# Wave 1 of an attention and MLP kernel: its casts, loads, weight sums and half products in another order

## The chip, the cores and the metric

One NeuronCore of a Trainium2 chip runs the kernel. Its engines work through instruction queues of their own, each in program order: TensorE (PE, matmuls), VectorE (DVE), ScalarE (ACT), GpSimd (POOL) and SyncE (SP, which here only issues DMAs). The metric is device time in microseconds of one execution. Before the change three runs took 203.18, 204.46 and 204.54 us; the median is 204.46.

## What is computed

Attention with a decay over 4 batches, 8 heads, 768 positions and 64 dimensions a head, then an MLP with a sigmoid GELU over the 3072 tokens:

```python
for b in range(nb):                                  # blocks of 64 positions
    intra = (q_b @ k_b^T * Dmask) @ v_b              # Dmask = lam ** (i - j), lower triangle
    inter = (q_b * lam_pow) @ kv_state
    out[:, :, block b] = intra + inter
    kv_state = lam_block * kv_state + (k_b * rev_pow)^T @ v_b
x = out as 3072 tokens x 512
h = x @ w_in                                         # 512 x 2048
g = h * sigmoid(1.702 * h)
out = g @ w_out                                      # 2048 x 512
```

## The kernel before

The sequence is cut into six waves of 128 positions (times 4 batches: 512 tokens a wave). For each wave the kernel loads k, q and v in two chunks c = 0, 1, scales and casts k and q to bf16 (`do_cast`), turns them (`turn_pe` through TensorE, `turn_dma` through SP's DMA transpose), computes scores, masks, outputs and state, and has the wave's attention output in `xT`. The first product of the MLP gives `h`, GELU gives `g_sb`, the second product (`product`, line 459) gives the output.

Both products of the later waves use a scheme with seven half products in place of eight (a Strassen-Winograd form). It needs sums and differences of halves of the inputs:

- `weight_sums(j)` (lines 421 to 426), for each of the four w_out chunks j: four VectorE instructions of 128x512 bf16. The first (t1) and the third (in place in w_out) read w_out alone, the second (t2) needs t1, the fourth (t4) needs t2.
- `g_sums` (line 439): s1 to s4 of `g_sb`, in a lower half (l) and an upper half (h), 128x1024 bf16 each.
- `in_sums` and `x_sums` (lines 518, 527) for the first product; "third" is an in-place one.

The second product's seven half products have numbers: 1 (raw inputs), 2, 3, 4 (t4), 5 (s1, t1), 6 (s2, t2), 7 (s3 and the in-place sum). Products 1, 6, 5, 3 add up in one PSUM bank, X; 2 goes to Q; 7 and 4 to V. Between 1, 6 and 5 the bank is copied to SBUF on ScalarE (`part`, line 472), so 6 and 5 may write X only when the copy before them is done; 4 waits likewise for the copy of 7; 3 waits until VectorE has read X after 5 (line 483).

The order of all work is written out by hand (`tc.manual_schedule`). Each engine runs its instructions in the order in which the program issues them. Wave 0 runs plain matmuls (fc 4 to fc 15 are `mlp1` calls, entries 3 to 14 of the list `main`), then half blocks of wave 1 (entries 15 to 22), then the steps of `STEPS[1]`. The list `side` says ahead of which entry of `main` the pieces of wave 1's attention and the sums are issued. In `STEPS`, `a1 a7 ...` and `b1 ...` are half products of the first product, `A2` and so on their GELUs, `P10` is product 1, half 0 (eight matmuls), `K0 tk0` the cast of k chunk 0 on GpSimd and its DMA transpose, `W2` the weight sums of chunk 2, `gl1` s1's lower half, `S0 M0 m1` scores and masks, `Lw` and `Lk` loads, `T1` a third `in_sums`. A minus sign means the wave before (in `STEPS[1]`: wave 0), a plus sign the wave after.

Three gates order DMAs. `gate_sync` issues a tiny DMA on SP that reads a weight chunk: it waits until the chunk has landed, and the loads behind it on SP wait with it. Wave 1's loads stand behind w_in chunk 2 (line 687), wave 2's k and q behind w_out chunk 2 (`next_loads`). `gate_pool` does the same on GpSimd: the w_out DMAs stand behind wave 1's q of chunk 1 (`weights_out`). In GpSimd's queue they also stand behind the cast of k of chunk 1, given to GpSimd in `side` at 12.

Of the kernel before, what the change touches and what calls it, by code (L numbers as in the profile page):

```python
# [25 lines left out]
def kernel(  # L26
# [13 lines left out]
    nc = tc.nc  # L40
# [379 lines left out]

    def weight_sums(j):
        b = w_out_sb[j].rearrange("p (m two) (c d) -> p two c m d", two=2, c=2)
        t1, t2, t4 = (t[:, j * CW // 2 : (j + 1) * CW // 2] for t in TS)
        for o, x, y in ((t1, b[:, 0, 1], b[:, 0, 0]), (t2, b[:, 1, 1], t1),
                        (b[:, 0, 1], b[:, 1, 1], b[:, 0, 1]), (t4, b[:, 1, 0], t2)):
            nc.vector.tensor_tensor(o, x, y, op=SUB)  # L426
# [136 lines left out]
    def one_step(w, s):  # L563
# [33 lines left out]
        elif s[0] == "X":  # L597
            x_sums(x)
        elif s[0] == "G":
            gate_pool(x_sum[w][3][0:1, 0, 0:1])  # L600
        elif s[0] == "g":
            m0, m1 = {"l": (0, 4), "h": (4, 8)}[s[1]]
            g_sums(w, m0, m1, tuple(int(c) - 1 for c in s[2:]))
        elif s[0] == "W":
            weight_sums(int(a))
        elif s[0] == "T":
            in_sums(int(a), True)
        elif s[0] == "L":
# [31 lines left out]
    with tc.manual_schedule():  # L640
# [42 lines left out]
        for j in range(3, len(IN_CH)):  # L683
            load_w_in(j)
        nc.gpsimd.affine_select(mask, mask, pattern=[[0, 1], [1, P]], channel_multiplier=-1, base=0,
                                compare_op=mybir.AluOpType.is_ge, fill=0.0)
        gate_sync(w_in_sb[2][0:1, 0, 0:2])
        load(1)
# [37 lines left out]
        def next_loads():  # L726
# [7 lines left out]
        side = [  # L734
            (0, end, 0, 1), (5, in_sums, 1), (6, in_sums, 2), (6.5, do_cast, 1, 0, "k", nc.vector), (7.5, in_sums, 3),
            (8.5, do_cast, 1, 0, "q", nc.vector), (9.5, turn_pe, 1, 0, "k"), (10.5, in_sums, 0),
            (11.5, turn_pe, 1, 0, "q"), (11.6, cast_v, 1, 0, (pool_copy, act_copy)),
            (12, do_cast, 1, 1, "k", nc.gpsimd), (12.6, scores, 0), (13, weights_out,), (13.1, next_loads,),
            (13.5, do_cast, 1, 1, "q", nc.vector), (13.6, one, 0), (14, turn_pe, 1, 1, "k"), (14.6, even, 0),
            (15, turn_pe, 1, 1, "q"), (15, end, 1, 0), (15, scores, 1), (16, cast_v, 1, 1, (act_copy, act_copy)),  # L740
            (16.5, one, 1), (17.5, even, 1), (17.6, g_sums, 0, 0, 4, (2,)), (17.7, g_sums, 0, 4, 8, (2,)),
            (18, end, 1, 1), (18.5, x_sums, 1), (18.6, in_sums, 3, True), (18.7, in_sums, 0, True),
            (19.5, weight_sums, 0), (20.5, weight_sums, 1),
        ]
# [38 lines left out]
```

## Time and profile before

The profiled execution took 202.9 us; its span from the first to the last instruction is 201.2 us.

| what | when or how long (us) |
|---|---|
| fc 4 starts, fc 15 ends | 20.64, 35.90 |
| wave 1's half blocks start, wave 1's first product starts | 39.99, 50.18 |
| wave 0's second product starts, its product 3 starts | 57.82, 72.04 |
| w_in chunks 1, 2, 3, 4 land | 17.82, 20.36, 22.86, 24.80 |
| wave 1's loads are issued; k, q, v of chunk 0 and k of chunk 1 land | 21.27; 26.34, 27.84, 29.34, 30.86 |
| w_out DMAs are issued; land | 33.53; 39.07, 42.15, 45.47, 48.01 |
| wave 2's loads are issued; GpSimd's casts of them | 46.19; 50.35 to 52.59 and 54.63 to 61.07 |
| wave 1's scores 0 (line 335) | 75.62 |

How to read the lines below. A timeline line gives the start, how long the group lasted, the engine, the line of the kernel, the operation, out<-in with the tiles' names, the shapes, and how many instructions of the kind followed each other; in brackets, how long the engine had been idle and who released it. The end of a matmul is modelled, so a wait reckoned from start to start is some 0.16 us longer than the bracket. Line 2 of the page is the busy share in 40 slices of about 5 us, in tenths, 9 for 90% or more.

### The profile page before, as it was taken

The numbers are of one execution on the slowest core, as the hardware profiler recorded it, in microseconds if no ns is written. First come the engines' busy times: TensorE is split into PE (matmuls) and PEld (weight loads), VectorE is DVE, ScalarE is ACT, GpSimd is POOL, SyncE is SP. The second block draws the span as 40 slices with busy tenths as digits, with TensorE's granted clock in tenths as the row PEclk, the third lists the DMA queues.
The fourth block names the chain that finished last, engine by engine and source line by source line (L and its number), as shares of the span: only waits on it lengthen the run. The fifth ranks groups of instructions, "written<-read, shape, count | busy, mean of one in ns | idle before, by whom it ended". The sixth has DMA issues, their size and how long they took to land.

```text
span 201.2 us, 5580 instructions
## 1 busy us (share of the span) xinstructions
PE 187.3 (93%) x2297; PEld 152.6 (76%) x2297; DVE 156.6 (78%) x293; ACT 130.8 (65%) x245; POOL 50.6 (25%) x73
## 2 busy tenths in 40 slices
PE   7999987779897889999999999999999999999993
PEld 2567534468775768888888888888988888888882
DVE  1797279767999784887979978979988799689860
ACT  4857667666791116647989548887559796487721
POOL 4564018200591000009600049200087000000000
PEclk9999999999999999999999999999999999999999
DMA  4999996999970798986799775699745831210013
GB/s 143 331 246 202 249 307 203 174 190 196 262 126 8 176 261 185 231 202 145 119 207 242 176 221 142 146 255 239 201 151 113 198 67 54 106 52 3 26 54 131
DMA packets 89603, 33.91 MB, mean 169 GB/s; under 512 B 67434, under 2 KB 89450, under 8 KB 89578
## 3 DMA queue, kind: packets, MB, share of 16 engines
q1 hardware_dynamic: 84680, 28.84, 57.7%
q0 software_dynamic: 4896, 4.72, 14.2%
q8 instruction: 18, 0.29, 0.6%
q14 instruction: 7, 0.06, 0.1%
q10 hardware_dynamic: 2, 0.00, 0.0%
HBM read 27.26 MB, written 6.29 MB: 167 GB/s over the span
## 4 chain that ended last, share of the span: by engine, by line
PE 70%; DVE 15%; DMA 6%; ACT 4%; POOL 2%; issue 1%; ACTq 0%; DVEq 0%
PE ps_X L459 20%; PE ps_hX L542 15%; PE ps_V L459 11%; PE ps_hV L542 7%; PE ps_Q L459 4%; DMA w_in<-in_moe_w_in_dram 4%; PE ps_hQ L542 4%; DVE w_out_t L426 4%; DMA kf<-in_k_dram 3%; DVE w_in_t L518 3%; PE ps_o L390 2%; PE ps_s L335 2%; PE ps_fill L147 2%; DVE qs L202 2%; DVE sm L267 1%; POOL ks L202 1%
## 5 line engine op out<-in xcount | busy, mean ns | idle before, releaser
L459 PEld LDWEIGHTS <-g_s 128*128 128x128 bf16 x384 | 37.1, 98 | 7.8 <-issue 2.9
L561 ACT ACTIVATE g_sb<-h_sb 128x512 bf16<-128x512 f32 x54 | 32.7, 633 | 1.4 <-DVE h_sb L550 1.4
L542 PEld LDWEIGHTS <-w_in 128*128 128x128 bf16 x288 | 28.2, 98 | 4.8 <-issue 1.5
L459 PEld LDWEIGHTS <-g_sb 128*128 128x128 bf16 x288 | 27.5, 98 | 5.0 <-issue 1.0
L221 ACT COPY part<-ps_hX 128x512 f32<-128x512 f32 x32 | 18.3, 588 | 10.3 <-PE ps_hX L542 10.3
L459 PE MATMUL ps_X<-w_out_t,g_s 128*128 128x256 bf16 x192 | 23.0, 273 | 0.7 <-ACT part L472 0.7
L542 PEld LDWEIGHTS <-w_in_t 128*128 128x128 bf16 x216 | 21.1, 98 | 2.5
L542 PE MATMUL ps_hX<-x_s,w_in_t 128*128 128x256 bf16 x144 | 21.6, 272 | 0.0
L439 DVE TENSOR_TENSOR g_s<-g_sb 128x1024 bf16<-128x1024 bf16 x24 | 16.2, 685 | 4.9 <-ACT g_sb L561 4.9
L209 POOL TENSOR_TENSOR ks<-kf,k_pow 128x512 bf16<-128x512 f32 x16 | 16.5, 1052 | 13.8 <-PE ps_h L414 13.8
L635 POOL CAST behind_q<-x_s 1x1 f32<-1x1 bf16 x3 | 0.5, 173 | 69.2 <-DVE x_s L527 69.2
L209 POOL TENSOR_TENSOR qs<-qf,q_pow 128x512 bf16<-128x512 f32 x16 | 16.6, 1063 | 2.0 <-DMA qf<-in_q_dram 2.0
L472 ACT COPY part<-ps_X 128x512 f32<-128x512 f32 (+1 forms) x14 | 7.3, 523 | 12.7 <-PE ps_X L459 12.2
L550 DVE TENSOR_TENSOR h_sb<-part,ps_hX 128x512 f32<-128x512 f32 x18 | 12.3, 681 | 2.9 <-ACT g_sb L561 1.9
L348 DVE SCALAR_TENSOR_TENSOR sm<-ps_s,inv_pow,mask 128x512 bf16<-128x512 f32 x16 | 11.2, 744 | 3.5 <-PE ps_s L335 3.5
L218 DVE COPY part<-ps_hV 128x512 f32<-128x512 f32 x16 | 11.0, 688 | 3.2 <-PE ps_hV L542 3.2
L481 ACT COPY o_sb<-ps_X 128x512 f32<-128x512 f32 (+1 forms) x7 | 3.7, 525 | 15.1 <-PE ps_X L459 15.1
L550 DVE TENSOR_TENSOR h_sb<-part,ps_hV 128x512 f32<-128x512 f32 x18 | 12.3, 684 | 1.1 <-PE ps_hV L542 1.0
L459 PE MATMUL ps_V<-w_out_t,g_sb 128*128 128x256 bf16 x96 | 11.6, 273 | 0.8 <-ACT part L472 0.8
L550 DVE TENSOR_TENSOR h_sb<-part,ps_hQ 128x512 f32<-128x512 f32 x18 | 12.2, 679 | 0.2 <-ACT part L221 0.2
L459 PE MATMUL ps_X<-w_out,g_s 128*128 128x256 bf16 x96 | 11.4, 272 | 1.0 <-DVE o_sb L483 1.0
L459 PE MATMUL ps_V<-w_out,g_s 128*128 128x256 bf16 x96 | 11.6, 272 | 0.7 <-DVE w_out L426 0.7
(112 smaller groups left out, 372.3 us busy)
## 6 DMA issues: line engine op xcount, KB each, us to landing
kf<-in_k_dram SPq DMA_DIRECT2D x10, 512.0 KB, 5.9
qf<-in_q_dram SPq DMA_DIRECT2D x10, 512.0 KB, 6.5
vf<-in_v_dram SPq DMA_DIRECT2D x10, 512.0 KB, 6.0
out_dram<-o_sb SPq DMA_DIRECT2D x24, 128.0 KB, 2.4
out_dram<-o_sb SPq DMA_DIRECT2D x12, 256.0 KB, 2.1
w_out<-in_moe_w_out_dram POOLq DMA_DIRECT2D x4, 512.0 KB, 9.1
kf<-in_k_dram SPq DMA_DIRECT2D x4, 256.0 KB, 4.0
qf<-in_q_dram SPq DMA_DIRECT2D x4, 256.0 KB, 4.6
```

The lines of the kernel that those rows point to most:

```text
L202: eng.tensor_tensor(x.rearrange("p a (r i j d) -> p r j i a d", i=2, j=2, d=D)[:, R, j], f[:, h].rearrange("p i (a d) -> p i a d", a=2), p ...
L209: eng.tensor_tensor(x.rearrange("p b (r i j d) -> p j (b r) i d", i=2, j=2, d=D)[:, j], f.rearrange("p h (a d) -> p (h a) d", a=2).rearran ...
L218: nc.vector.tensor_copy(out, in_)
L221: nc.scalar.copy(out, in_)
L348: nc.vector.scalar_tensor_tensor(sm, s, inv_pow[:, n : n + 1], mask.to_broadcast([P, B, P]), op0=MUL, op1=MUL)
L426: nc.vector.tensor_tensor(o, x, y, op=SUB)
L439: nc.vector.tensor_tensor(o, x, y, op=f)
L459: nc.tensor.matmul(bank[:, t], x[:, m, t * P : (t + 1) * P], y, start=(n in (1, 2, 7) and t == ts[0] * last and m == 0), stop=(m == FFC // ...
L472: nc.scalar.copy(part[w, n, t.start][:, t], bank[:, t])
L542: nc.tensor.matmul(bank[:, u], z[:, kc], y[:, kc], start=(n in (1, 2, 7) and u + kc == 0), stop=(kc == 1), skip_group_check=True)
L550: nc.vector.tensor_tensor(h, h_part[w, g, {2: 1, 5: 7, 4: 6}[n]], bank, op=ADD)
L561: nc.scalar.activation(g_of[w][:, a : b + 1 : b - a, 256 * i : 256 * i + 256], bank, GELU)
```

## The change

Casts and loads: wave 1's loads wait for w_in chunk 1 in place of 2. VectorE casts k of chunk 1 and GpSimd q of chunk 1 (before: the other way round). The q turn of chunk 0 comes one fc earlier, the turns, outputs and state of chunk 0 move against fc 14 and fc 15, the v casts of chunk 1 come ahead of the second q turn, and `in_sums` 0 moves from entry 10.5 to 14.9. Weight sums are issued by kind: of each chunk first instructions 1 and 3 (chunk 0 ahead of entry 20, chunks 1 to 3 between wave 1's first half products), then instruction 2 of all chunks behind product 1, instruction 4 of all chunks inside product 2. Wave 0's second product runs as 1 7 2 6 4 5 3 in place of 1 2 7 4 6 5 3, with wave 1's product 2 ahead of wave 0's product 3 and wave 1's product 1 ahead of wave 1's scores. `product` takes each PSUM bank when it first needs it, where it took all three at product 1, in every wave.

```diff
-    def weight_sums(j):
+    def weight_sums(j, which=(0, 1, 2, 3)):
...
-        for o, x, y in ((t1, b[:, 0, 1], b[:, 0, 0]), (t2, b[:, 1, 1], t1),
-                        (b[:, 0, 1], b[:, 1, 1], b[:, 0, 1]), (t4, b[:, 1, 0], t2)):
+        ops = ((t1, b[:, 0, 1], b[:, 0, 0]), (t2, b[:, 1, 1], t1),
+               (b[:, 0, 1], b[:, 1, 1], b[:, 0, 1]), (t4, b[:, 1, 0], t2))
+        for i in which:
+            o, x, y = ops[i]
             nc.vector.tensor_tensor(o, x, y, op=SUB)
...
-        if (w, "X", key) not in blocks:
-            for c in "QVX":
-                blocks[w, c, key] = acc(f"ps_{c}", shape=[P, 2, 256], tag="a" if last and ts[0] else "mm")
-        bank = blocks[w, CHAIN[n], key]
+        c = CHAIN[n]
+        if (w, c, key) not in blocks:
+            blocks[w, c, key] = acc(f"ps_{c}", shape=[P, 2, 256], tag="a" if last and ts[0] else "mm")
+        bank = blocks[w, c, key]
...
         elif s[0] == "W":
-            weight_sums(int(a))
+            for j in range(NCH) if a[0] == "*" else (int(a[0]),):
+                weight_sums(j, tuple(int(i) - 1 for i in a[1:]))
...
-        1: ("a1 a7 a2 a6 b1 b7 A2 a5 b2 b6 B2 a4 a3 b5 b4 A5 A4 b3 B4 B5 "
-            "W2 -P10 +K0 +tk0 -P11 W3 +Q0 +tq0 -P20 -P21 -gl1 -gl2 +K1 +tk1 -P70 -gh12 -P71 +Q1 +tq1 "
-            "gl3 gh3 -P40 -P41 +Lw T1 -P60 -P61 -gl4 -gh4 T2 -P50 -P51 gl1 gl2 gh12 -P30 -P31 "
-            "P20 P21 S0 S1 M0 P10 m1 Lk P11 v0 P70 P71 S2 S3 M2 m3 v1 o P40 P41 P60 gl4 gh4 P61 R P50 P51 "
+        1: ("a1 a7 a2 a6 b1 b7 A2 W113 a5 b2 b6 B2 a4 a3 W213 b5 b4 A5 A4 b3 W313 B4 B5 "
+            "-P10 +K0 +tk0 -P11 W*2 -gl1 -gl2 -P70 +Q0 +tq0 -P71 -gh12 -P20 W*4 -P21 +K1 +tk1 -P60 -P61 "
+            "+Q1 +tq1 +Lw gl3 gh3 -P40 -P41 -gl4 -gh4 -P50 T1 T2 -P51 P20 P21 -P30 -P31 gl1 gl2 gh12 "
+            "P10 S0 S1 M0 P11 m1 Lk v0 P70 P71 S2 S3 M2 m3 v1 o P40 P41 P60 gl4 gh4 P61 R P50 P51 "
             "+a1 X +a2 P30 P31 "),
...
-        gate_sync(w_in_sb[2][0:1, 0, 0:2])
+        gate_sync(w_in_sb[1][0:1, 0, 0:2])
...
-            (0, end, 0, 1), (5, in_sums, 1), (6, in_sums, 2), (6.5, do_cast, 1, 0, "k", nc.vector), (7.5, in_sums, 3),
-            (8.5, do_cast, 1, 0, "q", nc.vector), (9.5, turn_pe, 1, 0, "k"), (10.5, in_sums, 0),
-            (11.5, turn_pe, 1, 0, "q"), (11.6, cast_v, 1, 0, (pool_copy, act_copy)),
-            (12, do_cast, 1, 1, "k", nc.gpsimd), (12.6, scores, 0), (13, weights_out,), (13.1, next_loads,),
-            (13.5, do_cast, 1, 1, "q", nc.vector), (13.6, one, 0), (14, turn_pe, 1, 1, "k"), (14.6, even, 0),
-            (15, turn_pe, 1, 1, "q"), (15, end, 1, 0), (15, scores, 1), (16, cast_v, 1, 1, (act_copy, act_copy)),
-            (16.5, one, 1), (17.5, even, 1), (17.6, g_sums, 0, 0, 4, (2,)), (17.7, g_sums, 0, 4, 8, (2,)),
+            (0, end, 0, 1), (5, in_sums, 1), (6, in_sums, 2), (7.5, in_sums, 3), (8, do_cast, 1, 0, "k", nc.vector),
+            (8.5, do_cast, 1, 0, "q", nc.vector), (10, turn_pe, 1, 0, "k"), (10.5, do_cast, 1, 1, "k", nc.vector),
+            (11, turn_pe, 1, 0, "q"), (11.5, cast_v, 1, 0, (pool_copy, act_copy)), (11.6, do_cast, 1, 1, "q", nc.gpsimd),
+            (12, scores, 0), (12.5, weights_out,), (12.6, next_loads,), (13, one, 0), (13, turn_pe, 1, 1, "k"),
+            (14, even, 0), (14, end, 1, 0), (14, cast_v, 1, 1, (act_copy, act_copy)),
+            (14, turn_pe, 1, 1, "q"), (14.9, in_sums, 0), (15, scores, 1), (16.5, one, 1), (17.5, even, 1),
+            (17.6, g_sums, 0, 0, 4, (2,)), (17.7, g_sums, 0, 4, 8, (2,)),
             (18, end, 1, 1), (18.5, x_sums, 1), (18.6, in_sums, 3, True), (18.7, in_sums, 0, True),
-            (19.5, weight_sums, 0), (20.5, weight_sums, 1),
+            (19.5, weight_sums, 0, (0, 2)),
```

## The prediction, made before the changed kernel ran

> **What bounds the kernel now.** I read the page's busy rows first, then TensorE's timeline with its waits, then VectorE's and GpSimd's timelines side by side, then the DMA issues with their landings.
>
> ```profile
> PE 187.3 (93%) x2297; PEld 152.6 (76%) x2297; DVE 156.6 (78%) x293; ACT 130.8 (65%) x245; POOL 50.6 (25%) x73
> ...
> PE   7999987779897889999999999999999999999993
> ```
>
> TensorE (PE) is the bound; from 76 us on its row is 9 throughout and the chain of waits is all matmul. Only slices 5 to 15 (25 to 80 us) can give something. There TensorE's timeline shows these waits:
>
> ```profile
> 36.99 0.40 PE L238 MATMUL ps_t<-ident,qs 128*128 128x128 bf16 x4 [0.77 <-DVE qs L202]
> ...
> 54.20 0.60 PE L542 MATMUL ps_hQ<-xT,w_in 128*128 128x256 bf16 x4 [0.79 <-DVE h_sb L550]
> ...
> 61.31 0.82 PE L459 MATMUL ps_V<-w_out,g_s 128*128 128x256 bf16 x6
> 62.87 1.25 PE L459 MATMUL ps_V<-w_out,g_s 128*128 128x256 bf16 x10 [0.74 <-DVE w_out L426]
> 64.80 1.91 PE L459 MATMUL ps_V<-w_out_t,g_sb 128*128 128x256 bf16 x16 [0.67 <-ACT part L472]
> 66.54 1.91 PE L459 MATMUL ps_X<-w_out_t,g_s 128*128 128x256 bf16 x16
> 69.18 1.91 PE L459 MATMUL ps_X<-w_out_t,g_s 128*128 128x256 bf16 x16 [0.73 <-ACT part L472]
> 72.04 1.91 PE L459 MATMUL ps_X<-w_out,g_s 128*128 128x256 bf16 x16 [0.95 <-DVE o_sb L483]
> ```
>
> The four last brackets are wave 0's second product. Start to start 16 matmuls take 1.75 us (0.109 each: 66.54 to the 68.29 at which the next could have begun), so by starts the four cost 0.90, 0.84, 0.89 and 1.11: 3.74 us. Now the two engines that share the elementwise work:
>
> ```profile
> 57.85 1.13 DVE L426 TENSOR_TENSOR w_out_t<-w_out 128x512 bf16<-128x512 bf16 x1
> 59.01 1.15 DVE L426 TENSOR_TENSOR w_out_t<-w_out,w_out_t 128x512 bf16<-128x512 bf16 x1
> 60.09 1.26 DVE L426 TENSOR_TENSOR w_out<-w_out 128x512 bf16<-128x512 bf16 x1
> ```
>
> ```profile
> 56.64 2.05 POOL L209 TENSOR_TENSOR ks<-kf,k_pow 128x512 bf16<-128x512 f32 x2
> 58.66 2.41 POOL L209 TENSOR_TENSOR qs<-qf,q_pow 128x512 bf16<-128x512 f32 x2
> ```
>
> A weight sum takes 0.42 us where GpSimd rests (62.73) and 1.13 to 1.26 beside its casts, about one sum for each cast instruction: each seems to wait for a whole cast instruction. The adds that read PSUM (0.68 to 0.69 at 54.90 to 57.25, also beside casts) don't suffer.
>
> **The change part by part.**
>
> *Loads asked sooner.* w_in chunk 1 lands at 17.82 (11.69 + 6.1), chunk 2 at 20.36, so wave 1's loads are issued 2.54 us sooner. But the transfers have no room: chunk 3 follows chunk 2 by 2.5 us (lands 22.86), that is 1 MB of f32 read in 2.5 us, 0.42 MB/us, and the loads alone move 0.5 MB in 1.5 us (27.84 to 29.34), 0.35 MB/us, without a pause until 34.36. What is owed until then is the same, so the last loads gain 0 and the first 0 to 2.5. I take the first k at 24.8 to 26.3 and the others as before (q 27.84, second k 30.86, second q about 32.6, between its neighbours 30.86 and 34.36). If chunk 3 pays for it by half its rate it lands at about 24.0; fc 9 needs it at 20.64 + 5 x 0.87 = 25.0, so it costs nothing.
>
> *Wave 1's casts and turns.* First k: up to 0.86 us of TensorE's wait at 27.18 may go, but the q turn now stands one fc earlier and needs q at 27.84 + 1.5: fc 12 starts at 29.6 either way and is through at 30.45, where before fc 12 and the turn ended at 31.09: 0.65 gained. Scores 0 at 30.6, fc 13 done 32.1 (32.93 before). The second k cast goes to VectorE ahead of the four masks: 30.86 + 1.4 + 0.68 frees the first PSUM bank at 33.0, for which the k turn waits 0.6. fc 14 to 34.4; `seen` behind the kT copy (1.0) and GELU on ScalarE, 35.1; outputs and state 1.15, 36.25; the q turn finds GpSimd's cast done (32.6 + 2.4 = 35.0), so the 0.77 + 0.27 at 36.99 go. fc 15 to 37.6. In ScalarE's queue two v casts (1.1) now stand ahead of the qT copy: 35.8 + 0.5 + 1.1 + 0.95 = 38.35, a new wait of 0.8 for scores 1. First half of wave 1 at 39.2 (39.99 before). There the v casts pay back: the waits of 0.32 + 0.30 at 42.23 go, 0.8 by starts. So 1.6 gained at 44.2 (45.80) and wave 1's first product at 48.6 (50.18). in_sums 0, six instructions of 0.3, fits into VectorE's idle time ahead of the second masks (36.5 to 38.3).
>
> *GpSimd's queue.* The q cast (2.4) waits for q at 32.6, where the k cast waited for 30.86. Queued behind it are the four w_out issues: asked at 35.0 instead of 33.53, 0.8 to 1.7 later, I take 1.5. All that hangs on them moves by that: w_out chunks (39.1, 42.2, 45.5, 48.0 before), the gate for wave 2's loads, the casts of wave 2 (first k 50.35 to 51.85, first q 54.63 to 56.1).
>
> *Weight sums by kind.* Before, eight sums (48.95 to 53.5) stood ahead of the first h sum; now two do, and the 0.79 (0.95) at 54.20 goes. The pairs of chunks 1 and 2 lie between h sums; pair 2, ahead of b5's h sum, adds about 0.3 to the 0.55 (by starts) that b3 waited at 57.39. Second product at 55.6 (57.82 before): 2.2 gained.
>
> *The order 1 7 2 6 4 5 3.* It puts two products between each copy and its reuse, and wave 1's product 2 between 5 and 3: the waits at 64.80, 69.18 and 72.04 go, and 7 has its sums by 57.2. But 6 now comes fourth, due at 55.6 + 3 x 1.75 = 60.85, and needs all four t2 sums and four g sums (128x1024). VectorE is free for them at 55.7, just as wave 2's last six cast instructions begin. Ten VectorE instructions stand in line: two of chunk 3, four t2, four g sums. The first starts free (0.35); six are held by one cast each. A held weight sum costs 1.15. A held g sum is in no row: 0.68 if free, 1.9 if it scales as the weight sum does, 1.45 if it only waits as long and then adds its own 0.27 (0.68 - 0.42); I take 1.45, since the 57.85 to 60.09 rows step with the casts. 55.7 + 0.35 + 5 x 1.15 + 1.45 + 3 x 0.65 = 65.2. Product 6 starts at 63.95, when the lower half is there (a wait of 3.1), waits again in its middle for the upper one (0.85) and ends at 66.5. So 3.95 takes the place of the 3.74: the stall is late VectorE work again. [...] From 66.5: products 4, 5, wave 1's 2, and 3 run through (7.0): 73.5, where before the same set ended at 75.55.
>
> *After that* the work is the same and unwaited (0.17 at 80.57). The banks taken at need change nothing there: later waves start product 1 without a wait. Wave 2's transposes on SP stand behind product 2's output: its sum now ends at 65.2 + 4 x 0.35 + 0.6 = 67.2, outputs 1.45, kT 1.4, qT landing 2.76 after issue: 72.8; scores need it at 74.4.
>
> **Sum.** 75.55 - 73.5 = 2.0 us off the profiled execution's 202.9 (span 201.2): 200.9. The median of the runs is 204.46, 1.56 above the profiled one; the gain is taken from it: **202.5**. Its own range is a gain of 0.8 to 3.2 (q landing 0.9 sooner or later sums; since at most six casts can hold sums, the end of product 6 moves by less than 1 us): 201.3 to 203.7.
>
> **Rivals.**
> - *The sums are in time.* If the loads win their 2.5 us after all, or wave 2's casts fall beside PSUM adds, the waits of product 6 shrink: without any, 2.2 + 3.74 = 5.9 gained, 198.5; with half, 200.5. For it: casts at 54.63 to 57 hurt nothing before. Against: no pause in the transfers. 0.25.
> - *Slower: the scores of wave 2 wait.* Place: SP, where both transposes wait for an output whose sum moves from 63.07 to 66.6 us; the margin falls from 6.1 to 1.6 us. Bounds: 2.76 each, or 5.7 as the kT at 52.62 took beside loads; both at 5.7 make it 4.3 late past the margin, 202.5 + 4.3 = 206.8. It decides from a qT later than 74.4 and makes the kernel slower from 76.4 on. Against: at 65.38 and 66.80 they took 2.76 in the same company. 0.10.
> - *TensorE's clock falls.* In the first 6 us, 512 column matmuls are 0.43 apart (three in 1.46 at 3.73), at 9.91 they are 0.22: an array that had rested ran at half pace. Product 6's wait of 3.1 would be its longest since. [...] Today's waits are all near 1 or less. 0.05.
> - What I have not seen in wave 1's order, costing over 4 us against the sum: 0.08.
>
> **How the numbers follow.** What can be told from no change is about 1%, 2.0 us: faster is below 202.4, slower above 206.5. The forecast (0.52) straddles the first bound: 0.22 faster, 0.30 same. The first rival adds 0.25 faster; the transposes 0.06 same and 0.04 slower, the clock 0.05 same, the unseen 0.08 slower. Faster 0.47, same 0.41, slower 0.12. The range 199.5 to 205.2 leaves out the best third of the first rival and the ends of the slow ones, about 0.2.
>
> **What would show it.** Right: no brackets at 64.80, 69.18, 72.04's places; one wait of about 3 us ahead of product 6 ended by VectorE's g_s; w_out asked near 35; weight sums of 1.15 in step with casts; first half of wave 1 near 39, second product near 55.6. Wrong: w_out asked before 33.5, product 6 without a wait, scores of wave 2 ended by a transpose, or 512 column matmuls 0.43 apart after 60.

## The result, and the profile after

| | before | after |
|---|---|---|
| median of 20 executions (us) | 203.75 (202.98 to 205.45) | 204.97 (203.85 to 207.91) |
| ratio after/before | | 1.005, 95% interval 1.0029 to 1.0072 |

The change makes the kernel half a per cent slower. That is small but clear of the noise; the time lies inside the range (199.5 to 205.2), but the forecast, 202.5, was a gain. The execution profiled first (207.91 us) is one of those more than 1.5% above the fastest of their kernel, which are left out of all ratios and means (its w_in chunk 3 and its first k landed 2.3 to 2.4 us later), so the lines below come from a second profile of the same kernel: 204.85 us, span 203.2. In it `product` is line 461, `weight_sums` 428, `g_sums` 441, the copy to `part` 474. The scores of line 335 that start at 75.62 before are wave 2's: the step `S0` takes the wave after, with or without a sign. So the new order puts half 0 of wave 1's product 1 ahead of wave 2's scores, and the masks `m1` of those scores behind its half 1.

The page's busy rows and the clock in slices:

```profile
PE 188.1 (93%) x2297; PEld 153.2 (75%) x2297; DVE 156.7 (77%) x293; ACT 130.5 (64%) x245; POOL 51.6 (25%) x73
...
PE   7997979799983899899999999999999999999993
...
PEclk9999999999999699999999999999999999999999
```

TensorE's hole has moved to slice 12 (the 3), and one slice behind it has a clock of 0.6 of full. Before, the clock row had nines only:

```profile
PEclk9999999999999999999999999999999999999999
```

TensorE's timeline:

```profile
56.43 0.60 PE L544 MATMUL ps_hX<-x_s,w_in 128*128 128x256 bf16 x4 [0.86 <-DVE h_sb L552]
56.87 1.91 PE L461 MATMUL ps_X<-w_out,g_sb 128*128 128x256 bf16 x16
58.62 1.91 PE L461 MATMUL ps_V<-w_out,g_s 128*128 128x256 bf16 x16
60.36 1.91 PE L461 MATMUL ps_Q<-w_out,g_sb 128*128 128x256 bf16 x16
63.79 0.61 PE L461 MATMUL ps_X<-w_out_t,g_s 128*128 128x256 bf16 x4 [1.52 <-DVE g_s L441]
66.69 2.25 PE L461 MATMUL ps_X<-w_out_t,g_s 128*128 128x256 bf16 x12 [2.30 <-DVE g_s L441]
68.73 2.86 PE L461 MATMUL ps_V<-w_out_t,g_sb 128*128 128x256 bf16 x16
71.43 1.91 PE L461 MATMUL ps_X<-w_out_t,g_s 128*128 128x256 bf16 x16
...
74.92 1.91 PE L461 MATMUL ps_X<-w_out,g_s 128*128 128x256 bf16 x16
...
82.50 1.91 PE L461 MATMUL ps_V<-w_out_t,g_sb 128*128 128x256 bf16 x16 [0.96 <-ACT part L474]
```

The old brackets ahead of products 4, 5 and 3 are gone. In their place product 6 (63.79 and 66.69) waits 1.52 and 2.30. Then 28 matmuls, twelve of product 6 and the sixteen of product 4, take from 66.69 to 71.43, 4.74 us where 28 x 0.109 = 3.05 would do. The last line is wave 1's product 4, which waits 0.96 where before it waited 0.17:

```profile
80.57 1.91 PE L459 MATMUL ps_V<-w_out_t,g_sb 128*128 128x256 bf16 x16 [0.17 <-ACT part L472]
```

Who held product 6, on VectorE and then on GpSimd:

```profile
57.69 3.13 DVE L428 TENSOR_TENSOR w_out_t<-w_out,w_out_t 128x512 bf16<-128x512 bf16 x4
60.74 1.53 DVE L441 TENSOR_TENSOR g_s<-g_sb 128x1024 bf16<-128x1024 bf16 x1
62.31 1.42 DVE L441 TENSOR_TENSOR g_s<-g_s,g_sb 128x1024 bf16<-128x1024 bf16 x1
63.65 1.53 DVE L441 TENSOR_TENSOR g_s<-g_sb 128x1024 bf16<-128x1024 bf16 x1
65.22 1.42 DVE L441 TENSOR_TENSOR g_s<-g_s,g_sb 128x1024 bf16<-128x1024 bf16 x1
66.56 1.42 DVE L428 TENSOR_TENSOR w_out_t<-w_out,w_out_t 128x512 bf16<-128x512 bf16 x4
```

```profile
58.13 2.42 POOL L209 TENSOR_TENSOR qs<-qf,q_pow 128x512 bf16<-128x512 f32 x2 [3.17 <-DMA qf<-in_q_dram]
60.50 2.68 POOL L209 TENSOR_TENSOR ks<-kf,k_pow 128x512 bf16<-128x512 f32 x2
63.15 2.94 POOL L209 TENSOR_TENSOR qs<-qf,q_pow 128x512 bf16<-128x512 f32 x2
```

While GpSimd casts, a g sum takes 1.42 to 1.53 us. Free, it takes 0.68 (68.50 in this profile). Of the four weight sums at 57.69 the last two are held, 1.27 and 1.26; the last four (66.56, casts over) take 0.42 each, their spans overlapping slightly.

The windows of the same profile (length, busy time of each engine, granted clock, share of DMA, GB/s):

```profile
60.42:63.83 3.41, 1.89 (x18) 1.46 (x17) 3.38 (x4) 0.58 (x1) 3.41 (x4) 1.00 0.38 80
63.83:67.25 3.42, 1.12 (x9) 0.77 (x10) 3.38 (x5) 0.00 (x0) 2.26 (x2) 1.00 0.00 0
67.25:70.66 3.41, 3.41 (x19) 2.43 (x17) 2.53 (x6) 0.58 (x1) 0.00 (x0) 0.50 0.16 37
70.66:74.07 3.41, 3.41 (x33) 3.06 (x32) 2.37 (x5) 0.00 (x0) 0.00 (x0) 1.00 0.85 193
```

The first number behind the length is TensorE's busy time. Behind the 3.42 us in which it is busy for 1.12, the clock is 0.50 for 3.41 us (67.25 to 70.66), then 1.00 again.

### The profile page after: what moved, and what is told of

Its sections match the earlier page's. It is cut to its first block, busy times and chain, and to the rows that moved or that the text cites. A ratio compares the mean times of both kernels' runs of the same rounds, so it can differ in the third digit from the quotient of the medians.

```text
span 206.2 us, 5574 instructions
## 1 busy us (share of the span) xinstructions
PE 188.5 (91%) x2292; PEld 153.7 (75%) x2297; DVE 156.7 (76%) x293; ACT 130.6 (63%) x245; POOL 50.9 (25%) x73
## 4 chain that ended last, share of the span: by engine, by line
PE 73%; DMA 10%; DVE 8%; ACT 5%; issue 1%; SPq 1%; POOL 1%; ACTq 0%; DVEq 0%
PE ps_X L461 20%; PE ps_hX L544 14%; PE ps_V L461 9%; PE ps_hV L544 7%; PE ps_h L414 5%; PE ps_Q L461 4%; DMA vf<-in_v_dram 4%; DMA kf<-in_k_dram 4%; PE ps_hQ L544 4%; DVE w_out_t L428 3%; DMA qf<-in_q_dram 2%; DVE g_s L441 2%; PE ps_o L390 2%; PE ps_s L335 2%; DVE h_sb L552 1%
## 5 line engine op out<-in xcount | busy, mean ns | idle before, releaser
L461 PEld LDWEIGHTS <-g_s 128*128 128x128 bf16 x384 | 37.7, 100 | 9.6 <-DVE g_s L441 4.3
L461 PEld LDWEIGHTS <-g_sb 128*128 128x128 bf16 x288 | 28.2, 100 | 5.5 <-issue 0.9
L461 PE MATMUL ps_X<-w_out_t,g_s 128*128 128x256 bf16 x192 | 24.8, 285 | 3.5 <-DVE g_s L441 3.5
L441 DVE TENSOR_TENSOR g_s<-g_sb 128x1024 bf16<-128x1024 bf16 x24 | 17.1, 721 | 4.9 <-ACT g_sb L563 4.9
L209 POOL TENSOR_TENSOR qs<-qf,q_pow 128x512 bf16<-128x512 f32 x16 | 17.1, 1094 | 2.6 <-DMA qf<-in_q_dram 2.6
L461 PE MATMUL ps_V<-w_out_t,g_sb 128*128 128x256 bf16 x96 | 12.8, 289 | 1.0 <-ACT part L474 1.0
L221 ACT CAST v_sb<-vf 128x1024 bf16<-128x1024 f32 (+1 forms) x14 | 11.9, 867 | 0.9 <-DMA vf<-in_v_dram 0.8
L461 PE MATMUL ps_X<-w_out,g_sb 128*128 128x256 bf16 x96 | 12.3, 273 | 0.0
L461 PE MATMUL ps_Q<-w_out,g_sb 128*128 128x256 bf16 x96 | 12.0, 273 | 0.0
```

What stands on the lines that cost most here:

```text
L209: eng.tensor_tensor(x.rearrange("p b (r i j d) -> p j (b r) i d", i=2, j=2, d=D)[:, j], f.rearrange("p h (a d) -> p (h a) d", a=2).rearran ...
L221: nc.scalar.copy(out, in_)
L441: nc.vector.tensor_tensor(o, x, y, op=f)
L461: nc.tensor.matmul(bank[:, t], x[:, m, t * P : (t + 1) * P], y, start=(n in (1, 2, 7) and t == ts[0] * last and m == 0), stop=(m == FFC // ...
```

## The experiments

All ratios are to the kernel before, run on the same chips. Where the text speaks of the mean granted clock, 1.00 (0.996 or more) is an execution without a half paced stretch, 0.99 one with one stretch, 0.98 one with two: the profile before has 0.998 and no such stretch, the second profile 0.992 and 3.41 us at 0.50, the first 0.983 and 6.83 us at 0.50 (67.10 to 73.93).

**The changed kernel again**, for a profile.

> The changed kernel as it is, for a profile with no disturbed load and as the mark for the other three of this call. Theories: (clock) the wait ahead of wave 0's product 6 (3.2 us in the first profile) lets TensorE's clock fall to one half for one or two stretches of 3.4 us, which costs 1.4 to 3 us and eats the 2 us that the new order gains; (loads) the earlier asked loads and the casts in their new order cost the time, ahead of 50 us; (order) the order 1 7 2 6 4 5 3 itself loses, by its late sums, with no part for the clock. All three expect a ratio of about 1.005 here. Clock: a wait of 3 us and half clock behind it in this profile too, first half of wave 1 near 39 to 40, second product near 55.6 to 57. Loads: first half of wave 1 later than 40.

Measured: 204.73, ratio 1.0033 (1.0004 to 1.0063); its profile is the one above. All ten executions had a clock of 0.983 to 0.992.

**Keep TensorE busy in product 6's wait.**

```diff
+        elif s[0] == "Z":
+            z = acc("ps_keep", shape=[P, W])
+            for _ in range(int(a)):
+                nc.tensor.matmul(z, ident, w_out_sb[0][:, 0, :], start=True, stop=True)
...
-            "-P10 +K0 +tk0 -P11 W*2 -gl1 -gl2 -P70 +Q0 +tq0 -P71 -gh12 -P20 W*4 -P21 +K1 +tk1 -P60 -P61 "
+            "-P10 +K0 +tk0 -P11 W*2 -gl1 -gl2 -P70 +Q0 +tq0 -P71 -gh12 -P20 W*4 -P21 +K1 +tk1 Z10 -P60 -P61 "
```

> The changed kernel with ten matmuls of 512 columns (2.2 us) that nothing needs, issued inside the wait ahead of product 6. Clock: the clock stays at full, product 6 starts when it did, and the kernel is 1.4 to 3 us faster than the changed one: ratio to the kernel before 0.990 to 0.998. Loads and order: no change against the changed kernel, ratio about 1.005.

Measured: 204.79, ratio 1.0027 (0.9998 to 1.0056). Windows of its profile:

```profile
26.45:29.86 3.41, 1.63 (x13) 0.76 (x12) 2.31 (x7) 1.17 (x3) 0.00 (x0) 1.00 1.04 306
29.86:33.28 3.42, 3.42 (x26) 1.74 (x28) 1.77 (x6) 2.38 (x4) 0.61 (x1) 0.50 0.96 282
...
63.99:67.40 3.41, 2.17 (x12) 0.80 (x9) 3.34 (x6) 0.00 (x0) 0.47 (x1) 1.00 0.00 0
```

The clock stays full behind product 6's wait, where 2.17 of 3.41 us are now busy (product 6's last twelve matmuls take 1.32 us), and is 0.50 behind the k turn's wait instead (1.63 of 3.41). The edit works where it was put. Half of the executions kept the full clock throughout: five average 204.61, and the six with one stretch 204.57. With everything else as it is, the full clock alone brings nothing here; the profile (0.99) shows a new wait of 0.77 for a transpose of wave 3, at 105.98.

**One half of the change each.** With the old products: before's weight sums and product order, the rest changed.

```diff
-        1: ("a1 a7 a2 a6 b1 b7 A2 W113 a5 b2 b6 B2 a4 a3 W213 b5 b4 A5 A4 b3 W313 B4 B5 "
-            "-P10 +K0 +tk0 -P11 W*2 -gl1 -gl2 -P70 +Q0 +tq0 -P71 -gh12 -P20 W*4 -P21 +K1 +tk1 -P60 -P61 "
-            "+Q1 +tq1 +Lw gl3 gh3 -P40 -P41 -gl4 -gh4 -P50 T1 T2 -P51 P20 P21 -P30 -P31 gl1 gl2 gh12 "
-            "P10 S0 S1 M0 P11 m1 Lk v0 P70 P71 S2 S3 M2 m3 v1 o P40 P41 P60 gl4 gh4 P61 R P50 P51 "
+        1: ("a1 a7 a2 a6 b1 b7 A2 a5 b2 b6 B2 a4 a3 b5 b4 A5 A4 b3 B4 B5 "
+            "W21234 -P10 +K0 +tk0 -P11 W31234 +Q0 +tq0 -P20 -P21 -gl1 -gl2 +K1 +tk1 -P70 -gh12 -P71 +Q1 +tq1 "
+            "gl3 gh3 -P40 -P41 +Lw T1 -P60 -P61 -gl4 -gh4 T2 -P50 -P51 gl1 gl2 gh12 -P30 -P31 "
+            "P20 P21 S0 S1 M0 P10 m1 Lk P11 v0 P70 P71 S2 S3 M2 m3 v1 o P40 P41 P60 gl4 gh4 P61 R P50 P51 "
...
-            (19.5, weight_sums, 0, (0, 2)),
+            (19.5, weight_sums, 0), (20.5, weight_sums, 1),
```

> The changed casts, loads and turns of wave 1, with the weight sums and the second product in the order of before (1 2 7 4 6 5 3). Clock: no wait of 3 us, no fall; worked out by the rows of before the set of products ends 1.7 us sooner than before: ratio about 0.992. Order: the same, 0.990 to 0.995. Loads: slower than before, ratio about 1.005 or more.

Measured: 202.70, ratio 0.9927 (0.9897 to 0.9958).

With the old casts: before's list `side` and its gate on w_in chunk 2, with the new weight sums and products.

```diff
-        gate_sync(w_in_sb[1][0:1, 0, 0:2])
+        gate_sync(w_in_sb[2][0:1, 0, 0:2])
...
-            (0, end, 0, 1), (5, in_sums, 1), (6, in_sums, 2), (7.5, in_sums, 3), (8, do_cast, 1, 0, "k", nc.vector),
...
+            (0, end, 0, 1), (5, in_sums, 1), (6, in_sums, 2), (6.5, do_cast, 1, 0, "k", nc.vector), (7.5, in_sums, 3),
...
```

> The casts, loads and turns of before, with the changed weight sums and the second product as 1 7 2 6 4 5 3. Clock: GpSimd's casts run 1.5 us sooner against the products and product 1 starts 2.5 us later than in the changed kernel, so product 6 waits about 0.6 and then 0.85, the clock stays at full and the kernel gains about 2 us: ratio about 0.990. Loads: faster than before as well, 0.990. Order: product 6's waits stay long and the ratio is 1.00 to 1.01.

Measured: 203.41, ratio 0.9985 (0.996 to 1.0009). Neither half is slower by itself; only both together are. Product 6 waits 0.47 and 0.72, near what was expected, but the gain of 2 us didn't come. In its profile (mean clock 0.997) no stretch at half pace shows, and product 3 ends at 74.06 where before it ended at 75.55 with wave 1's product 2: 1.5 gained. All of that is given back in two later waits (the first was 0.17 before, the second is new), on TensorE's timeline:

```profile
79.89 1.91 PE L461 MATMUL ps_V<-w_out_t,g_sb 128*128 128x256 bf16 x16 [0.96 <-ACT part L474]
104.34 0.51 PE L335 MATMUL ps_s<-qT,kT 64*128 64x128 bf16 x12 [0.82 <-DMA qT<-qs]
```

**The gate alone**, back on w_in chunk 2, in the changed kernel and in the one with the old products.

```diff
-        gate_sync(w_in_sb[1][0:1, 0, 0:2])
+        gate_sync(w_in_sb[2][0:1, 0, 0:2])
```

> The changed kernel with one edit undone: wave 1's loads wait again for w_in chunk 2. Theory A (asking sooner makes the first load later, because its transfers share the queues with w_in chunks 3 and 4): the first k lands near 26.5 us although it is asked 2.5 us later (27.7 in the changed kernel), w_in chunk 4 near 25 in place of 27, the w_out DMAs are asked near 35.3 in place of 36.3, product 6's whole wait shrinks from 3.8 to about 2.8 us and the second product starts about 0.7 sooner; ratio 0.993 to 0.998. Rival (the earlier ask is harmless, w_in's late landing is chance): landings within 0.4 us of the changed kernel's and ratio 1.003.

> The same undoing of the gate in the kernel with the new casts and the old product order (ratio 0.993 so far). Theory A: another 0.5 to 1.0 us off, ratio 0.988 to 0.990. Rival (gate harmless): 0.993.

Measured: 204.53, ratio 1.0048 (1.0017 to 1.008), and 202.81, ratio 0.9963 (0.9939 to 0.9987). With the old products the median is that of the early gate (202.70) to 0.1 us. The theory's steps fail too: product 6 still waits 3.08 and 0.72, 3.8 together, and w_out is asked at 36.78. So asking sooner isn't what makes the kernel slower than before. A smaller loss isn't ruled out: sorted by clock the late gate is ahead, 202.17 (six at full clock) against 202.62 (ten) with the old products, 203.72 (four with one stretch) against 204.5 with the new ones, but more of its executions had a stretch, or a second one, and these groups ran on different chips. The rival's landings weren't right either. Loads asked 3.2 us later (22.89, behind a chunk 2 that itself came 0.7 later than in the changed kernel's profile) brought the first k 0.4 us later, at 28.15. Reckoned from the landing of w_in chunk 2, the first k comes 6.0 to 7.4 us later with the gate on 2 (four profiles), and 6.2 to 7.9 with the gate on 1 (eleven; two executions with late transfers are left out); chunk 4, asked together with chunk 3, comes 4.4 to 4.9 behind chunk 2 with the gate on 2 (6.0 in the one where both were asked 0.9 late) and 5.7 to 7.0 with the gate on 1. The earlier request delays the weights and brings the first k no sooner. Nor do they share a queue, as the theory had it: between 18 and 40 us of the second profile the loads' 3.15 MB go through q1, the weights through q0.

**The two casts swapped back.**

```diff
-            (8.5, do_cast, 1, 0, "q", nc.vector), (10, turn_pe, 1, 0, "k"), (10.5, do_cast, 1, 1, "k", nc.vector),
-            (11, turn_pe, 1, 0, "q"), (11.5, cast_v, 1, 0, (pool_copy, act_copy)), (11.6, do_cast, 1, 1, "q", nc.gpsimd),
+            (8.5, do_cast, 1, 0, "q", nc.vector), (10, turn_pe, 1, 0, "k"), (10.5, do_cast, 1, 1, "k", nc.gpsimd),
+            (11, turn_pe, 1, 0, "q"), (11.5, cast_v, 1, 0, (pool_copy, act_copy)), (11.6, do_cast, 1, 1, "q", nc.vector),
```

> The changed kernel with k of chunk 1 cast on GpSimd and q of chunk 1 on VectorE, as before. Nothing else is moved. Theory B (product 6's wait comes from GpSimd's late queue: the cast of q and the w_out DMAs behind it): w_out is asked near 34.7 (k1's landing 32.3 and 2.4 for the cast) in place of 36.3, wave 2's casts run 1.6 us sooner, product 6's two waits together fall from 3.8 to about 2.2 us and the clock no longer falls behind it; ratio 0.990 to 0.997. Rival (the wait comes from VectorE's count of sums, whatever GpSimd's casts do): waits within 0.4 us of 3.8, the half pace stays, ratio 1.00 or more.

Measured: 204.74, ratio 1.0044 (1.0013 to 1.0075). Product 6's waits fell to 0.47 and 0.72, but by the wrong way: the second product started at 60.23 in place of 56.87, because the k cast now stood ahead of a v copy in GpSimd's queue (1.83 of wait ahead of a state matmul) and b3 waited 1.86 for its h sum. Product 6's second part began at 67.43, against 66.69 in the changed kernel: its end follows the sums, not TensorE. The edit moved more than it was meant to, so the GpSimd theory stays untested by it.

**Full clock.** The unneeded matmuls of the second run and five more ahead of the k turn.

```diff
+        def keep_busy(n):
+            z = acc("ps_keep", shape=[P, W])
+            for _ in range(n):
+                nc.tensor.matmul(z, ident, xT[0][:, 0, :], start=True, stop=True)
...
-            (8.5, do_cast, 1, 0, "q", nc.vector), (10, turn_pe, 1, 0, "k"), (10.5, do_cast, 1, 1, "k", nc.vector),
+            (8.5, do_cast, 1, 0, "q", nc.vector), (9.9, keep_busy, 5), (10, turn_pe, 1, 0, "k"), (10.5, do_cast, 1, 1, "k", nc.vector),
```

> The changed kernel with unneeded matmuls in both long waits: ten of 512 columns ahead of product 6 and five ahead of wave 1's first k turn; their results are not used. Theory C (half a clock for 3.4 us is what the changed kernel loses against its two halves): no half pace anywhere from 10 us to the end, 1.7 us less than the 204.7 of the changed kernel, so about 203.0, ratio 0.996. Rival (the clock is a bystander: the time is set by VectorE's and GpSimd's late work, and a stretch at half pace is made up in the waits that follow): 204.5 to 204.8, ratio 1.003, though the clock stays full. A third case: the fall moves to yet another wait (2 to 3 us from a turn or a score), then the ratio is 1.003 and the test says nothing on the price.

Measured: 204.19, ratio 1.0033 (1.0011 to 1.0056). Nine of twelve executions had a clock of 1.00, mean 204.04. Twenty-two executions of the changed kernel with one stretch average 204.5, eighteen with two 205.3. So the full clock brought 0.5 us against one stretch (on another chip), not the expected 1.7. Its profile shows one place where time was lost again, on TensorE's timeline:

```profile
104.66 0.51 PE L335 MATMUL ps_s<-qT,kT 64*128 64x128 bf16 x12 [0.37 <-DMA qT<-qs]
```

and SP's queue shows why a transpose of wave 3 can be late:

```profile
68.45 1.42 SPq L491 DMA_DIRECT2D out_dram<-o_sb  x2
...
72.78 2.42 SPq L88 DMA_DIRECT2D vf<-in_v_dram  x2
...
95.08 3.91 SPq L245 DMA_TRANSPOSE kT<-ks  x2
99.52 2.75 SPq L245 DMA_TRANSPOSE qT<-qs  x2
```

Before, product 2's output was issued at 63.78 and wave 3's first kT at 92.87. Now the output stands behind a sum that waits for the late sums ahead of it in VectorE's queue, and SP is still 2 us behind at wave 3 (95.08 against 92.87). In the profiles where TensorE is late too, by a half paced stretch behind product 6, no wait for this transpose shows (wave 3's scores at 105.85 in the second profile, sixteen in a row without a bracket).

**Product 2's sum and output behind wave 2's transposes and v loads**, in the changed kernel and with the full clock.

```diff
-            if n == 2 and 0 < w < NW - 1:
+            if n == 2 and w < NW - 1:
...
-            "+Q1 +tq1 +Lw gl3 gh3 -P40 -P41 -gl4 -gh4 -P50 T1 T2 -P51 P20 P21 -P30 -P31 gl1 gl2 gh12 "
+            "+Q1 +tq1 +Lw -o gl3 gh3 -P40 -P41 -gl4 -gh4 -P50 T1 T2 -P51 P20 P21 -P30 -P31 gl1 gl2 gh12 "
```

> The changed kernel with one edit: the sum and the output of wave 0's product 2 are issued behind wave 2's transposes and v loads. SP then no longer holds these behind an output whose sum stands behind ten late sums in VectorE's queue. Theory D (SP's late queue is the second part of the loss): the v loads are asked near 69 us in place of 72.9, the wait of 0.96 ahead of wave 1's product 4 falls to 0.2 or less, no wait for qT of wave 3 near 105; product 6 still waits some 3.8 us and the clock falls behind it, so about 0.8 us off: 203.9, ratio 1.000. Rival (that wait belongs to ScalarE's own order, whenever v lands): 0.96 stays and the time with it, 1.003.

> The same edit in the kernel with unneeded matmuls in both long waits (the full clock; their results are not used). Theory: the two losses add up: full clock 0.5 and SP's two waits 1.2 (0.8 at wave 1's product 4 and 0.4 for qT near 105), so 203.0, ratio 0.996 to 0.997, which is what the sum of the prediction without clock and SP would be, less what GpSimd's later queue costs. Rival (something else holds the rest): ratio 1.000 or more with both waits gone.

Measured: 205.09, ratio 1.0056 (1.0026 to 1.0086), and 203.19, ratio 0.994 (0.9908 to 0.9971). The v loads come ahead of the output in both:

```profile
66.17 2.43 SPq L88 DMA_DIRECT2D vf<-in_v_dram  x2
68.70 9.11 SPq L491 DMA_DIRECT2D out_dram<-o_sb  x8
...
93.24 3.19 SPq L245 DMA_TRANSPOSE kT<-ks  x2
```

(this is the one with the full clock). There the wait near 105 is gone and 1.3 us with it (executions at clock 1.00: 202.75 against 204.04, of which the one profile above shows 0.37; the rest is not resolved; the two ran on different chips, on which the kernel before at full clock averages 203.67 and 203.60). Alone, the edit brings nothing: with one stretch 204.53, where the changed kernel on the same chip has 204.45. That the half clock covers what SP gains is read from these two results together, not shown by itself. The wait of 0.96 ahead of wave 1's product 4 stays in both, though the v loads are asked 6 to 7 us sooner. It is not the loads, and theory D is wrong on that point.

**The changed kernel beside these on the same chip.**

> The changed kernel as it is, beside the three others on the same chip: 204.7 to 205.0, ratio 1.003 to 1.005, every execution with one or two stretches of 3.41 us at half a clock.

Measured: 205.04, ratio 1.0062 (1.0027 to 1.0097); six executions at 0.99 and six at 0.98, none at 1.00.

**Work in product 6's wait.** Wave 1's product 2 ahead of wave 0's 6, product 1 between wave 0's 5 and 3, product 2's output later.

```diff
-            blocks[w, c, key] = acc(f"ps_{c}", shape=[P, 2, 256], tag="a" if last and ts[0] else "mm")
+            blocks[w, c, key] = acc(f"ps_{c}", shape=[P, 2, 256], tag="a" if last and ts[0] or (w, c) == (1, "Q") else "mm")
...
-            "-P10 +K0 +tk0 -P11 W*2 -gl1 -gl2 -P70 +Q0 +tq0 -P71 -gh12 -P20 W*4 -P21 +K1 +tk1 -P60 -P61 "
-            "+Q1 +tq1 +Lw gl3 gh3 -P40 -P41 -gl4 -gh4 -P50 T1 T2 -P51 P20 P21 -P30 -P31 gl1 gl2 gh12 "
-            "P10 S0 S1 M0 P11 m1 Lk v0 P70 P71 S2 S3 M2 m3 v1 o P40 P41 P60 gl4 gh4 P61 R P50 P51 "
+            "-P10 +K0 +tk0 -P11 W*2 -gl1 -gl2 -P70 +Q0 +tq0 -P71 -gh12 -P20 W*4 -P21 +K1 +tk1 P20 P21 -P60 -P61 "
+            "+Q1 +tq1 +Lw -o gl3 gh3 -P40 -P41 -gl4 -gh4 -P50 T1 T2 -P51 P10 P11 -P30 -P31 gl1 gl2 gh12 "
+            "S0 S1 M0 m1 Lk v0 P70 P71 S2 S3 M2 m3 v1 o P40 P41 P60 gl4 gh4 P61 R P50 P51 "
```

> The changed kernel with product 2's output later as before, and with wave 1's product 2 ahead of wave 0's product 6 (its bank is one of the five others) and wave 1's product 1 between wave 0's products 5 and 3 in its place. The wait of product 6 is filled with 1.75 us of work that is needed anyway. Theory (the end of product 6 is set by GpSimd's casts and VectorE's sums, not by TensorE): product 6 still ends near 68, 1.75 us of work are then already done, the window is too little idle for the clock to fall; 2.5 to 3 us off the changed kernel's 204.7: 202.0, ratio 0.990. Rival (product 6 is pushed back by what stands ahead of it): ratio 0.998 to 1.003.

Measured: 200.62 (five executions, 200.39 to 200.86), ratio 0.9844 (0.9816 to 0.9873): faster than both kernels. Its TensorE timeline:

```profile
59.94 3.66 PE L461 MATMUL ps_Q<-w_out,g_sb 128*128 128x256 bf16 x32
64.22 0.61 PE L461 MATMUL ps_X<-w_out_t,g_s 128*128 128x256 bf16 x4 [0.62 <-DVE g_s L441]
66.40 1.48 PE L461 MATMUL ps_X<-w_out_t,g_s 128*128 128x256 bf16 x12 [1.57 <-DVE g_s L441]
67.72 1.91 PE L461 MATMUL ps_V<-w_out_t,g_sb 128*128 128x256 bf16 x16
...
78.19 1.91 PE L461 MATMUL ps_V<-w_out_t,g_sb 128*128 128x256 bf16 x16 [0.36 <-ACT part L474]
```

Product 6's second part begins at 66.40, as in the changed kernel (66.69), but sixteen more useful matmuls stand ahead of it (x32 at 59.94), and product 6's last twelve take 1.32 us (66.40 to 67.72), full pace. The mean clock is 0.997 or more in all five. The edit moved three things at once: product 2, product 1 with the masks, and product 2's output.

**The masks ahead of product 1's second half.** After the loads were ruled out, ScalarE's own order was left. In the changed kernel's ScalarE timeline:

```profile
79.28 0.58 ACT L474 COPY part<-ps_X 128x512 f32<-128x512 f32 x1 [1.78 <-PE ps_X L461]
79.76 1.27 ACT L344 ACTIVATE sm<-ps_s,inv_pow 128x512 bf16<-128x512 f32 x2
80.91 1.05 ACT L221 CAST v_sb<-vf 128x1024 bf16<-128x1024 f32 x1
81.84 0.61 ACT L474 COPY part<-ps_V 128x512 f32<-128x512 f32 x1
```

Copy, masks, v cast and the copy that product 4 waits for stand in one row behind product 1's end. Scores 0 and 1 were done at 78.2, so the masks could have begun 1.1 us before the copy. In the kernel before they did: `m1` was issued ahead of product 1's second half, now behind it. ScalarE before:

```profile
76.28 1.27 ACT L344 ACTIVATE sm<-ps_s,inv_pow 128x512 bf16<-128x512 f32 x2 [1.67 <-PE ps_s L335]
78.13 0.59 ACT L472 COPY part<-ps_X 128x512 f32<-128x512 f32 x1 [0.59 <-PE ps_X L459]
```

```diff
-            "P10 S0 S1 M0 P11 m1 Lk v0 P70 P71 S2 S3 M2 m3 v1 o P40 P41 P60 gl4 gh4 P61 R P50 P51 "
+            "P10 S0 S1 M0 m1 P11 Lk v0 P70 P71 S2 S3 M2 m3 v1 o P40 P41 P60 gl4 gh4 P61 R P50 P51 "
```

> The changed kernel with one step moved: the split masks m1 (two ScalarE instructions) are issued ahead of the second half of wave 1's product 1 again, as in the kernel before, so ScalarE does them before it waits for product 1's end. Theory E (the wait of 0.96 ahead of wave 1's product 4 is ScalarE's queue: copy of product 1, masks, v cast, all behind product 1's end): the bracket falls to about 0.2, the time by 0.7 to 0.8: 204.2, ratio 1.001 to 1.002. Rival (ScalarE is late for another reason, or the time comes back in a later wait): 0.96 stays, or goes and the ratio stays at 1.005.

Measured: 203.67, ratio 0.9999 (0.9967 to 1.003). ScalarE now, and the wait on TensorE:

```profile
80.80 1.26 ACT L344 ACTIVATE sm<-ps_s,inv_pow 128x512 bf16<-128x512 f32 x2 [0.80 <-PE ps_s L335]
81.95 0.58 ACT L474 COPY part<-ps_X 128x512 f32<-128x512 f32 x1
```

```profile
84.22 1.91 PE L461 MATMUL ps_V<-w_out_t,g_sb 128*128 128x256 bf16 x16 [0.17 <-ACT part L474]
```

The 0.96 is 0.17 again, and the whole comes out 0.5 us faster than was expected, which is within the interval. The half clock is still there in every execution (0.98 or 0.99).

**All three taken out:** full clock, output 2 later, masks first.

> The changed kernel with the three suspected losses taken out together: full clock by unneeded matmuls in both long waits (results not used), product 2's output behind wave 2's transposes and loads, masks m1 ahead of product 1's second half. Theory: the three add up to what the prediction missed; the second product ends near 75 us, nothing waits behind it, 203.2 - 0.8 = 202.4, ratio 0.989 to 0.992, which is the gain of the prediction's sum. Rival (a fourth loss): 0.994 or more although all three waits are gone.

Measured: 203.16, ratio 0.9962 (0.9925 to 1.0). The twelve executions fall into two groups: six at clock 1.00, mean 202.1, and six at 0.992, mean 203.7. So here, with the two other losses out, executions with one half paced stretch are 1.6 us longer, and those without are 1.4 us faster than the kernel before at full clock (203.49, twenty executions on the same chip). The whole, 203.16, lies in the range of the rival. The unneeded matmuls didn't prevent the fall every time; where it fell in those six isn't known, as the one profile is of a full clock (with the gate on w_in chunk 2, 22 matmuls from 19.79 on took 4.04 us, where 22 x 0.109 = 2.40 would do). Its product 6 and what comes after:

```profile
61.79 2.32 PE L612 MATMUL ps_keep<-w_out,ident 128*128 128x512 bf16 x10
65.17 0.61 PE L461 MATMUL ps_X<-w_out_t,g_s 128*128 128x256 bf16 x4 [1.06 <-DVE g_s L441]
66.50 1.48 PE L461 MATMUL ps_X<-w_out_t,g_s 128*128 128x256 bf16 x12 [0.71 <-DVE g_s L441]
...
79.85 1.91 PE L461 MATMUL ps_V<-w_out_t,g_sb 128*128 128x256 bf16 x16 [0.17 <-ACT part L474]
```

**Scores earlier in the fastest version.**

```diff
-            "+Q1 +tq1 +Lw -o gl3 gh3 -P40 -P41 -gl4 -gh4 -P50 T1 T2 -P51 P10 P11 -P30 -P31 gl1 gl2 gh12 "
-            "S0 S1 M0 m1 Lk v0 P70 P71 S2 S3 M2 m3 v1 o P40 P41 P60 gl4 gh4 P61 R P50 P51 "
+            "+Q1 +tq1 +Lw -o gl3 gh3 -P40 -P41 -gl4 -gh4 -P50 T1 T2 -P51 P10 S0 S1 M0 m1 P11 -P30 -P31 gl1 gl2 gh12 "
+            "Lk v0 P70 P71 S2 S3 M2 m3 v1 o P40 P41 P60 gl4 gh4 P61 R P50 P51 "
```

> The kernel with wave 1's product 2 in product 6's wait, and now wave 2's first scores with their masks between the halves of wave 1's product 1, ahead of wave 0's product 3. Theory E: the remaining 0.36 ahead of wave 1's product 4 goes, 0.2 to 0.4 us less than 200.6: 200.3, ratio 0.983. Rival: the scores wait for a transpose or a bank in the earlier place and it is 0.5 us or more slower.

Measured: 201.78, ratio 0.9878 (0.9845 to 0.9912). The wait of 0.36 fell to 0.17 without a new one, but seven of the ten compared executions had a stretch at half pace (mean 201.9; the three at full clock 200.6, as the version before it). In its profile (mean clock 0.989), an execution with late w_in chunks (chunk 4 at 30.36), that stretch is over by 21.03, long before the edit: from there 24 matmuls take 2.68 us, 0.112 each. Product 6 waits 1.63 and 0.72, and its last twelve matmuls take 1.32 us, full pace. Needed work in that wait didn't keep the clock from falling elsewhere. Inconclusive on the 0.2 us.

## Why the prediction was wrong

The forecast's span was 201.2 - 2.0 = 199.2; the second profile has 203.15. The 3.95 us between them are in these terms (they add up to 3.97, the sums being rounded):

| step of the prediction | predicted | second profile | off by |
|---|---|---|---|
| second product starts | 55.6 | 56.87 | 1.27 |
| product 6's waits (by starts) | 3.95 | 1.68 + 2.46 = 4.14 | 0.19 |
| rest of product 6 and product 4 at full pace | 3.05 | 4.74 | 1.69 |
| "After that the work is the same and unwaited" | +0 | 0.96 - 0.17, and 0.03 elsewhere | 0.82 |

The 202.5 itself stood on a median of three runs, 204.46; that of twenty was 203.75, so the same sum would have said 201.8.

- **Right: the stall becomes VectorE's late sums ahead of product 6.** The place, the releaser and the price of a held g sum (1.42 to 1.53, predicted 1.45) came as worked out. Two weight sums and four g sums were held, where five and one were predicted; as either loses some 0.7 to 0.85 to a cast, the total hardly changed. The g sums bear out the 1.45 against scaling (1.9). The waits behind the copies went as said.
- **Wrong: "the last loads gain 0 and the first 0 to 2.5".** The first k landed at 27.71, not 24.8 to 26.3. The sooner request was paid by w_in chunk 4 (27.07 where 24.80 was seen before), and the loads still came behind it. By their medians the gate experiments show no time in it either way, so this term is no gain rather than a loss; of the 1.27 at the second product's start, 0.81 was already there at fc 4 (21.45 against 20.64), which waited for w_in chunk 1 before the earlier request could matter. That part is chance, not the change.
- **Mis-sized: w_out "asked at 35.0 instead of 33.53".** It was 36.32, 2.8 late: GpSimd began its cast of q at 33.93, not 32.6. The sums still came out near the forecast, since six casts bound what can be held, as the prediction said.
- **Failed: "From 66.5: products 4, 5, wave 1's 2, and 3 run through (7.0)".** The rival that the clock falls (0.05) was what happened: in all 40 compared executions of the changed kernel the mean clock shows one stretch or two (0.982 to 0.992), and in its three profiles half pace begins at product 6's waits. The prediction judged by the length of one wait (3.1) and held it against "Today's waits are all near 1 or less". In the second profile that wait came as two waits with four matmuls between them, which leave TensorE 1.12 of 3.42 us busy. No run made before the prediction shows how long a fall for such a wait would last or what it would cost, so the 0.05 of this rival, counted as same, was the author's estimate; the runs showed 3.41 or 6.83 us at 0.50, and for one stretch a price of 1.69 in the profile and 1.6 in the run with all three losses out. Taken out alone it was worth 0 to 0.5.
- **Failed: "After that the work is the same and unwaited (0.17 at 80.57)".** With `m1` behind product 1's second half, that product's copy stands ahead of the masks on ScalarE. The prediction followed the move on TensorE, for which it is free, and not the other engine's instructions. It costs 0.8 by the bracket; undoing it alone brought the ratio from 1.005 to 0.9999.
- **Half right: "Slower: the scores of wave 2 wait" (0.10), for transposes on SP.** The cause was right: SP stood behind product 2's output, whose sum began at 67.90. Wave 2's scores never waited (qT landed at 74.38, scores at 77.64). The backlog came out one wave later, 0.37 to 0.82 us for wave 3's qT in four profiles, and in none where a half paced stretch came behind product 6.
- **"The sums are in time" (0.25)** was not seen in any run with the new casts and the new order.

With the three losses out and a full clock the change gains 1.4 us, where the forecast had 2.0. The working of the sum up to product 6 held in the main; what it left out cost more than it gained. The 0.6 that is still missing is near what the table has left, the second product's start beyond fc 4's (0.46) and product 6's longer waits (0.19), but no experiment takes these out.

What stays open: why the old casts with the new order wait so much less at product 6 is only read from the profile (w_out asked at 33.99, casts over sooner); the experiment meant to show it moved another copy.

## What to carry to other kernels

When waits are gathered into one place, add up TensorE's idle time over a few microseconds, not wait by wait: here two waits of 1.52 and 2.30 us close together were followed by 3.41 us at half the clock, the four of before (0.67 to 0.95 by bracket) by none. A step moved in a hand-written order has to be followed on every engine on which it issues something, the copy behind a matmul group included. Fill such a hole with work that is needed anyway: the version that did so, with two other losses out, was 2% faster than the changed kernel. At full clock it was 1.5 us faster (200.6 against 202.1) than the version with the same losses out and unneeded matmuls in the hole, on another chip. Removing waits one at a time mostly uncovered the next.

## What the hardware showed

- **In four profiles the clock fell behind a stretch in which TensorE waited, but was not idle, and was full again 3.41 or 6.83 us later.** In the second profile TensorE is busy for 1.12 of 3.42 us (33%) up to 67.25, and the clock is 0.50 from there to 70.66. In the first it is busy for 0.86 of 3.41 (25%) up to 67.10, and the clock is 0.50 to 73.93. With the gate on w_in chunk 2 it is busy for 0.61 of 3.42 (18%) up to 67.51, and with the first unneeded matmuls for 1.63 of 3.41 (48%) up to 29.86; in both the next 3.41 or 3.42 us have 0.50. The clock stayed full behind 1.89 of 3.41 (55%, second profile, up to 63.83), 2.43 of 3.41 (71%, gate on w_in chunk 2, up to 64.09) and 2.17 of 3.41 (64%, first unneeded matmuls, up to 67.40). Where between these a fall begins is not shown. Nearly the same two waits of the changed kernel (1.52 and 2.30; 1.52 and 2.29) were followed by one stretch in the second profile, where the 28 matmuls behind them take 4.74 us, and by two in the profile of its run beside the other kernels (mean clock 0.983), where they take 5.91; why is not shown either.
- **A half paced stretch cost less here where something else was late.** Executions with and without one lay 1.6 us apart (203.7 and 202.1) where the two other losses were out; with these in, the full clock was worth 0.5 in one kernel (204.04 against 204.5) and nothing in another (204.61 against 204.57). That the losses cover one another is read from these times, not traced.
- **Loads asked earlier arrived no earlier** in a stretch in which the DMA share is full (nine tenths and more from 5 to 30 us in the second profile): 6.2 to 7.9 us behind w_in chunk 2, against 6.0 to 7.4 when asked later. They delayed the weight chunk ahead of them by about 1 to 2 us.
